# The block tile is read ahead of T, T's corner is transposed at a place of its own, and the inverse runs from 0.42 to 1.10 of a unit's period

## Chip, core and metric

The kernel runs on one core of one Trainium2 chip. The metric is the device time of one execution in microseconds (us), lower is better; the kernel before has a median of 692.04 us in three runs (691.59 to 693.32).

## What is computed

A linear attention with the delta rule runs over 768 steps for 4 batches of 8 heads (head size 48); its output, as 3072 tokens of width 384, goes through two dense layers with a squared ReLU between them. The core of the reference:

```python
k_n = k / (np.linalg.norm(k, axis=-1, keepdims=True) + 1e-06)
for t in range(S):
    kt, vt, bt = (k_n[:, :, t], v[:, :, t], beta[:, :, t, None])
    y[:, :, t] = np.einsum('bhd,bhde->bhe', q[:, :, t], state)
    v_old = np.einsum('bhde,bhd->bhe', state, kt)
    state = state + bt[:, :, :, None] * np.einsum('bhd,bhe->bhde', kt, vt - v_old)
...
h = np.maximum(x @ w_in, 0.0)
return (h * h @ w_out).astype(np.float32)
```

## The kernel before

**Units.** The 768 steps are cut into 12 units of 64 (`C`), for all 32 batch-head pairs at once. Inside a unit the recurrence is a triangular system: a 64x64 matrix T per head, the inverse of "identity plus masked key products", turns (v minus what the state gives) into the solved values. T consists of two 32x32 diagonal blocks and one 32x32 corner.

**Blocks and inverse.** `static` makes the masked key products of a unit (tile `ap`) and writes the four 32x32 diagonal parts to a DRAM tile `blocks` (`to_blocks`, L387). `from_blocks` (L397) reads them back in another layout as the block tile `lt`, 512 KB with one buffer; the same last piece of `static` issues the loads of v (L247) and beta (L274, L276). `invert` inverts the diagonal blocks on VectorE (DVE) in 31 elimination steps, each a product (L541) and a subtraction (L542) on the tile `z`, and a last multiplication by beta (L544). It writes `z` to DRAM (`inv`, L548) and, when that has landed, reads it back twice: as T's diagonal parts into `tt` (L552, 4 issues) and as the corner factor `t1t` (L557, 4 issues).

**The corner and the state.** `whole` makes T's corner. DVE transposes `t1t` into `t1` (L587); TensorE (PE) multiplies `ap` with `tt` (L594), ScalarE (ACT) copies that to `m` (L596), `keys_on_state` multiplies keys with the state (L633) and DVE subtracts the result from v (`vt`, L641). Then PE multiplies `t1` with `m` (L607), ACT writes the result to `tt` (L611), and `queries_on_state` follows (L633 again, output `g`). Later come `solved` (L657), `scores_on_solved` (L671) and `keys_on_solved` (L689), after which DVE updates the state (L694).

**The dense layers.** `moe` runs for the unit before: its first product is L750, its second L737; ACT applies ReLU, square and a rounding (L757, L758, L760), DVE forms the remainders `h_l` (L729) and `x_l` (L720). These matmuls fill TensorE while the recurrence's chain goes on.

**Order.** The schedule is manual: every engine runs its instructions in the order in which the Python code emits them. For each unit's period the parts are generators, each with a list of places between 0 and 1; `weave` sorts all places and advances one generator at each. In period u the inverse of unit u+1 begins at `I0` = 0.47 and ends at `I1` - 1 = 0.14 of the next period; its reads of `inv` stand at 0.16, the last piece of `static` for unit u+2 at 0.165. The chain `two_visits` has its first place at 17.5/32 (all of `whole`) and its second at 25.5/32 (`solved` and what follows). All DMAs named here are issued by one engine's queue, SyncE (SP), in order; SP waits at an issue until what it needs has come.

The lines of the main loop that set these places:

```python
begun = J0 if u == 1 else I0
n_i = round((1 - begun) / (I1 - begun) * NI)
...
    parts.append((ahead, [-1, 0.165]))
...
    parts.append((inverse, steps(n_i, begun, 1)))
    left = steps(NI - n_i, 0, I1 - 1) + [0.16]
...
parts.append((chain, [x / STEPS for x in (CHAIN if u > 1 else CHAIN1)]))
```

Of the kernel before, what the change touches and what calls it, by code (L numbers as in the profile page):

```python
# [8 lines left out]
F32 = mybir.dt.float32  # L9
# [12 lines left out]
def kernel(  # L22
# [22 lines left out]
    nc = tc.nc  # L45
    B, H, S, D = q.shape
    DM, DF = w_in.shape
    P = 128
    C = 64
    HB = 32  # L50
# [11 lines left out]
    apool = ctx.enter_context(tc.tile_pool(name="attn", bufs=2))  # L62
# [179 lines left out]
    def load_to(dst, x, d, width, queues=None):  # L242

        if x is v:
            for b, src in enumerate(tokens(x, d)):
                for c in range(NC):
                    nc.sync.dma_start(out=dst[b * C:(b + 1) * C, c], in_=src[:, c])  # L247
            return
        for j, queue in enumerate(queues or (nc.sync, nc.sync)):
            for b, src in enumerate(tokens(x, d)):  # L250
                rows = slice((b ^ j) * C, (b ^ j) * C + C)
                for c in range(NC):
                    queue.dma_start(out=dst[rows, c, j::2, :width], in_=src[:, c, j::2])
# [24 lines left out]
    def load_v(d):  # L278
        d["vt"] = apool.tile([P, NC, H, D], F32, name="vt", bufs=2)
        load_to(d["vt"], v, d, D)  # L280
# [31 lines left out]
    def x_tile(u=2):  # L312

        turn[0] += 1
        pool, name = (ps_h, "h") if u <= 1 and split_early and turn[0] % 4 >= 2 else (ps_x, "x")
        return pool.tile([P, PC], F32, name=name)


    def static(d):

        u = d["u"]
# [68 lines left out]
        def from_blocks(blocks):  # L390

            d["lt"] = lt = apool.tile([P, HB, HB], F32, name="lt", bufs=1)
            if u <= 1:
                nc.sync.dma_start(out=lt, in_=shared["blocks"].rearrange("n u h s t -> (n u h) s t"))
                return
            for g in range(2):
                nc.sync.dma_start(out=lt[g * C:(g + 1) * C], in_=blocks.rearrange("n h s t -> (n h) s t"))  # L397
# [45 lines left out]
        blocks = to_blocks()  # L443
        yield
        from_blocks(blocks)
        load_v(d)
        if u + 1 < MERGED:
            load_q(ds_[u + 1])
# [74 lines left out]
    def invert(d):  # L523
# [32 lines left out]
        for n in range(4):  # L556
            nc.sync.dma_start(out=t1t[n * HB:(n + 1) * HB], in_=inv[n // 2 * 2].rearrange("(k j) s t -> j s k t", j=2)[n % 2])  # L557

    def whole(d):

        u, ap = d["u"], d["ap"]
        tt = ttile[u % 2]
        upper = [slice(b * C, b * C + HB) for b in range(2)]
        lower = [slice(b * C + HB, (b + 1) * C) for b in range(2)]

        if not u:

            low, t1 = d["low"], d["t1"]
            m = mpool.tile([P, H2, HB], F32, name="x_l", bufs=1)
            ps = ps_h.tile([P, PC], F32, name="h").rearrange("p (h t) -> p h t", h=H2)  # L570
            for h in range(H2):
                for b in range(2):
                    nc.tensor.matmul(ps[upper[b], h], lhsT=ap[lower[b], h // H, h % H, 0, :HB], rhs=low[lower[b], h],
                                     start=True, stop=True)
            for b in range(2):
                nc.scalar.copy(out=m[upper[b]], in_=ps[upper[b]])
            yield
            ps = x_tile(u).rearrange("p (h t) -> p h t", h=H2)
            for h in range(H2):
                for b in range(2):  # L580
                    nc.tensor.matmul(ps[upper[b], h], lhsT=t1[upper[b], h], rhs=m[upper[b], h], start=True, stop=True)
            for b in range(2):
                nc.scalar.mul(out=tt.rearrange("p c h t -> p (c h) t")[upper[b], :, HB:], in_=ps[upper[b]], mul=-1.0)
            yield
            return
        t1 = apool.tile([P, H, HB], F32, name="t1", bufs=1)
        nc.vector.transpose(out=t1, in_=d["t1t"])  # L587
        m = apool.tile([P, H, HB], F32, name="m", bufs=1)
        at = [upper, lower]
        ps = ps_h.tile([P, PC], F32, name="h")[:, :H * HB].rearrange("p (k t) -> p k t", k=H)  # L590
        for h in range(H2):
            c, e = h // H, h % H
            for b in range(2):
                nc.tensor.matmul(ps[at[h % 2][b], h // 2], lhsT=ap[lower[b], c, e, 0, :HB],  # L594
                                 rhs=tt[lower[b], c, e, HB:], start=True, stop=True)
        nc.scalar.copy(out=m, in_=ps)  # L596
        if u == 1:
            yield
        keys_on_state(d)
        if u < MERGED - 2:  # L600
            yield
        ps = [(x_tile(u) if u < MERGED - 2 else ps_h.tile([P, PC], F32, name="h"))[:, :H * HB]
              .rearrange("p (k t) -> p k t", k=H) for _ in range(2)]
        for h in range(H2):
            for b in range(2):
                rows = at[h % 2][b]
                nc.tensor.matmul(ps[h % 2][upper[b], h // 2], lhsT=t1[rows, h // 2], rhs=m[rows, h // 2], start=True, stop=True)  # L607
        right = tt.rearrange("p c (k j) t -> p j (c k) t", j=2)
        for j in range(2):
            for b in range(2):  # L610
                nc.scalar.mul(out=right[upper[b], j, :, HB:], in_=ps[j][upper[b]], mul=-1.0)  # L611
        if u == 1:
            yield
        queries_on_state(d)
        yield
# [20 lines left out]
    def keys_on_state(d):  # L636

        ks = areas([x_tile() for _ in range(2)], NP)
        on_state(d, 0, ks)
        for left, old in zip(by_parity(d["vt"]), ks):  # L640
            nc.vector.tensor_tensor(out=left, in0=left, in1=old, op=ALU.subtract)  # L641
# [147 lines left out]
    def steps(n, a, b):  # L789

        return [a + (b - a) * (m + 0.5) / n for m in range(n)]
# [27 lines left out]
    def prepared(u):  # L819

        yield from static(ds_[u])
# [13 lines left out]
    def two_visits(d, ahead):  # L835

        ahead = ahead or iter(())
        for _ in whole(d):
            pass
        take(ahead, 1)  # L840
        yield
        solved(d)
        take(ahead, 1)
        scores_on_solved(d)
        take(ahead, 1)
        if d["u"] < units - 1:
            keys_on_solved(d)
        yield
# [1 line left out]
    STEPS = 32  # L850
    OVER = 4
    MERGED = 4
    CHAIN = (17.5, 25.5)
    CHAIN1 = (14.4, 17, 19.5, 21.5, 23.5, 27)
    L1, N1, N2 = 0.01, (0.36, 0.76), (0.03, 0.42)
    I0, I1, NI = 0.47, 1.14, HB
    J0 = 0.54
    units = S // C
    ds_ = []
    split_early = True  # L860
# [3 lines left out]
    with tc.manual_schedule(engines=engines):  # L864
# [74 lines left out]
        corner, inverse = inverse, None  # L939
        for u in range(1, units):  # L940
            parts = []
            begun = J0 if u == 1 else I0
            n_i = round((1 - begun) / (I1 - begun) * NI)
            if inverse:
                parts.append((inverse, left))
            getting, now = loads(u), moe(ds_[u - 1]) if u > 1 else first
            parts += [(now, [-2])] if u > 1 else []
            if u < MERGED - 1:
                parts.append((static(ds_[u + 1]), [-1, 0.155, 0.165] if u > 1 else [0.12, 0.2, 0.21]))
            elif ahead:  # L950
                parts.append((ahead, [-1, 0.165]))
            ahead = prepared(u + 2) if 1 < u < units - 2 else None
            inverse = invert(ds_[u + 1]) if u < units - 1 else None
            if inverse:
                parts.append((inverse, steps(n_i, begun, 1)))
                left = steps(NI - n_i, 0, I1 - 1) + [0.16]
            if u == 1:
                parts.append((corner, [0.04, 0.09, 0.1]))
                parts.append((third, [0.01, 0.015, 0.03, 0.045]))
                parts.append((late_loads(), [0.08]))  # L960
                parts.append((splits, steps(3 * (NW - FIRST) + 3 - used, 0, 0.72)))
                parts.append((pair[1], [0.25]))
            parts.append((getting, [L1] + steps(6, *N2) + [0.72, 0.93] if u + 2 < units else []) if u > 1 else
                         (getting, [0.09] + steps(6, *N1) + [0.93, 0.94]))
            chain = two_visits(ds_[u], ahead) if u > 1 else state_part(ds_[u])
            parts.append((chain, [x / STEPS for x in (CHAIN if u > 1 else CHAIN1)]))
            if before:
                parts += [(before, [x / STEPS for x in range(OVER)] + [0.2, 0.21])]
            parts.append((now, [x / STEPS for x in range(OVER, STEPS)] if u > 1 else steps(STEPS - OVER, 0, 1)))
            weave(*parts)  # L970
            before = now
# [34 lines left out]
```

## Time and profile before

| | us |
|---|---|
| median of three runs | 692.04 |
| the profiled execution, its own time | 693.88 |
| its span (first to last instruction) | 692.2 |
| TensorE busy in the span | 611.9 (88%) |
| VectorE busy | 425.8 (62%) |
| ScalarE busy | 317.5 (46%) |
[...]

[...] "Unit 7's corner" means the stretch from 404 to 430 us, in which T of unit 7 comes back and its corner is made; the corners of units 2 to 11 stand some 46 to 54 us apart from each other. A DVE entry of one line number repeats for each step. POOL is GpSimd.

### The profile page before, as it was taken

To read this page: it belongs to the slowest core of one execution; us is meant where nothing else is said; L and a number is where in the kernel's file an instruction comes from. 1 tells how busy PE (TensorE), PEld (TensorE's weight loads), DVE (VectorE), ACT (ScalarE), POOL (GpSimd) and SP (SyncE) were. 2 spreads that over 40 slices of the span, in tenths; PEclk is the share of its full clock that TensorE was granted. 3 is DMA by queue.
4 is the path that set the end of the run, shared out by engine and by line. 5 is a ranking of instruction groups with operands and counts; after the bars stand their busy time and mean duration, and the time that the engine had idled before them with its cause. 6 is when DMAs were issued, how large, how long until landed. Compare 5 with 4: busy or idle time off the path is not lost.

```text
span 692.2 us, 23846 instructions
## 1 busy us (share of the span) xinstructions
PE 611.9 (88%) x10392; PEld 581.9 (84%) x10392; DVE 425.8 (62%) x1131; ACT 317.5 (46%) x621; POOL 29.8 (4%) x52
## 2 busy tenths in 40 slices
PE   2858798998997997997997997997997998998997
PEld 2456787998897997996997997997997998898997
DVE  4796698864864774774684684684685574651121
ACT  5648576544443444443453443453444343444352
POOL 4000100010010010010010010010010010000000
PEclk9957899998997998997998998997998998999999
DMA  7788552253144135135135235235135024020000
GB/s 230 173 260 222 118 99 38 42 99 65 26 74 82 26 59 94 29 54 96 32 48 98 36 47 97 38 48 95 34 48 92 3 42 91 3 46 19 24 1 24
DMA packets 172464, 49.32 MB, mean 71 GB/s; under 512 B 164288, under 2 KB 167368, under 8 KB 172360
## 3 DMA queue, kind: packets, MB, share of 16 engines
q1 hardware_dynamic: 168840, 47.06, 33.8%
q8 instruction: 82, 1.34, 0.8%
q10 hardware_dynamic: 3392, 0.72, 0.6%
q14 instruction: 22, 0.18, 0.1%
q0 software_dynamic: 128, 0.01, 0.0%
HBM read 36.54 MB, written 10.49 MB: 68 GB/s over the span
## 4 chain that ended last, share of the span: by engine, by line
PE 47%; DVE 19%; DMA 13%; SPq 10%; ACT 7%; issue 4%; ACTq 0%; DVEq 0%
PE o L737 18%; PE h L750 15%; DVE tmp L541 5%; DVE z L542 4%; DMA vt<-in_v_dram 4%; DMA inv<-z 4%; PE g L633 3%; SPq L557 3%; SPq L247 2%; DVE ap L379 2%; SPq L552 2%; PE g L671 2%; PE x L353 2%; DVE state L694 2%; DMA w<-in_moe_w_in_dram 2%
## 5 line engine op out<-in xcount | busy, mean ns | idle before, releaser
L737 PE MATMUL o<-w,h_h 128*128 128x384 f32 x768 | 209.1, 355 | 0.0
L750 PE MATMUL h<-x_h,w 128*128 128x256 f32 x1152 | 169.3, 283 | 0.0
L757 ACT ACTIVATE r<-h 128x512 f32<-128x512 f32 x96 | 57.5, 599 | 236.4 <-PE h L750 234.3
L729 DVE TENSOR_TENSOR h_l<-r,h_h 128x512 fp32r<-128x512 f32 x96 | 66.1, 689 | 146.9 <-ACT h_h L760 146.8
L750 PEld LDWEIGHTS h<-x_h,w 128*128 128x128 f32 x1152 | 155.4, 190 | 0.7
L737 PEld LDWEIGHTS o<-w,h_h 128*128 128x128 f32 x768 | 142.0, 197 | 2.6
L737 PE MATMUL o<-w,h_l 128*128 128x384 f32 x384 | 133.4, 347 | 0.0
L541 DVE SCALAR_TENSOR_TENSOR tmp<-lt,bt,z 128x126 f32<-128x126 f32 (+22 forms) x310 | 97.4, 314 | 47.7 <-DMA lt<-blocks 35.6
L750 PE MATMUL h<-x_l,w 128*128 128x256 f32 x576 | 99.9, 282 | 0.0
L542 DVE TENSOR_TENSOR z<-z,tmp 128x126 f32<-128x126 f32 (+22 forms) x310 | 79.2, 255 | 10.6
L750 PEld LDWEIGHTS h<-x_l,w 128*128 128x128 f32 x576 | 82.2, 190 | 0.0
L737 PEld LDWEIGHTS o<-w,h_l 128*128 128x128 f32 x384 | 75.2, 196 | 0.0
L758 ACT ACTIVATE r<-r 128x512 f32<-128x512 f32 x96 | 60.7, 632 | 3.1
L760 ACT CAST h_h<-r 128x512 fp32r<-128x512 f32 x96 | 59.5, 620 | 3.1
L607 PE MATMUL h<-m,t 32*32 32x32 f32 x640 | 10.3, 227 | 33.9 <-DVE t L587 33.0
L607 PEld LDWEIGHTS h<-m,t 32*32 32x32 f32 x640 | 9.1, 139 | 35.0 <-issue 34.4
L611 ACT ACTIVATE tt<-h 32x256 f32<-32x256 f32 x40 | 15.0, 374 | 39.7 <-PE h L607 39.2
L530 POOL MEMSET z<- 128x512 f32 x10 | 5.5, 546 | 505.5 <-DMA inv<-z 350.4
L694 DVE TENSOR_TENSOR state<-state,x 48x384 f32<-48x384 f32 x40 | 22.0, 550 | 3.7 <-PE x L689 3.1
L671 PE MATMUL g<-vt,ap 64*64 64x48 f32 x768 | 17.3, 221 | 6.4 <-ACT vt L659 5.4
L671 PEld LDWEIGHTS g<-vt,ap 64*64 64x64 f32 x768 | 14.5, 134 | 9.1 <-ACT vt L659 8.6
L633 PE MATMUL g<-state,kq 48*64 48x48 f32 x704 | 20.6, 290 | 1.4 <-issue 1.4
(147 smaller groups left out, 672.7 us busy)
## 6 DMA issues: line engine op xcount, KB each, us to landing
w<-in_moe_w_in_dram SPq DMA_DIRECT2D x12, 512.0 KB
w<-in_moe_w_out_dram SPq DMA_DIRECT2D x16, 384.0 KB
lt<-blocks SPq DMA_DIRECT2D x20, 256.0 KB
qpad<-in_q_dram SPq DMA_DIRECT2D x96, 48.0 KB
vt<-in_v_dram SPq DMA_DIRECT2D x48, 96.0 KB
out_dram<-a SPq DMA_DIRECT2D x46, 96.0 KB
kpad<-in_k_dram SPq DMA_DIRECT2D x88, 48.0 KB
blocks<-ap SPq DMA_DIRECT2D x40, 64.0 KB
```

The lines of the kernel that those rows point to most:

```text
L541: nc.vector.scalar_tensor_tensor(out=tmp, scalar=bt[:, s:s + 1], op0=ALU.mult, op1=ALU.mult, **factors)
L542: nc.vector.tensor_tensor(out=z[:, :nj, s + 1:], in0=z[:, :nj, s + 1:], in1=tmp, op=ALU.subtract)
L557: nc.sync.dma_start(out=t1t[n * HB:(n + 1) * HB], in_=inv[n // 2 * 2].rearrange("(k j) s t -> j s k t", j=2)[n % 2])
L633: nc.tensor.matmul(dst[j][to, c, p], lhsT=d["kq"][rows, c, p, b, x], rhs=state[rows, b, c, p], start=(c == 0 and p == 0) if x else True, s ...
L671: nc.tensor.matmul(gy[j][to, c, p], lhsT=ap[rows, c, h, 1], rhs=uu[rows, c, h], start=(u == 0 and c == 0 and p == 0), stop=True, skip_grou ...
L694: nc.vector.tensor_tensor(out=state[rows, b], in0=state[rows, b], in1=ku[b][rows], op=ALU.add)
L729: nc.vector.tensor_tensor(out=h_l, in0=r, in1=h_h.bitcast(F32), op=ALU.subtract)
L737: nc.tensor.matmul(o[i], lhsT=a[:, e, i * P:(i + 1) * P], rhs=halves["wo", ft][w], start=(ft == 0 and n == 0), stop=(ft == FT - 1 and n == 2))
L750: nc.tensor.matmul(hp[:, e], lhsT=halves["wi", (kt, ft // EACH)][w][:, f], rhs=x[:, kt], start=(n == 0), stop=(n == 3 * KT - 1))
L757: nc.scalar.activation(out=r, in_=hp, func=AF.Relu)
L758: nc.scalar.activation(out=r, in_=r, func=AF.Square)
L760: nc.scalar.copy(out=h_h, in_=r)
```

## The change

Three things are edited, all of them places in an order; no arithmetic is changed. (1) The last piece of `static` for units from 2 on is split: the read of the block tile is one piece, the loads of v, q and beta the next. The reads now stand at 0.13 of a period, the loads at 0.17, and T's reads at 0.15 (0.16 in period 2), so from unit 3 on SP issues the block tile ahead of T. (2) The transposition of `t1t` is a function of its own, `corner_rows`, that `two_visits` calls at a new place 15.5/32, before `whole` at 17.5/32. (3) The inverse begins at 0.42 and ends at 1.10 of a period (0.5 and 1.12 in period 2; 0.54 and 1.14 in period 1, as before).

```diff
         from_blocks(blocks)
+        yield
         load_v(d)
...
+    def corner_rows(d):
+
+        d["t1"] = apool.tile([P, H, HB], F32, name="t1", bufs=1)
+        nc.vector.transpose(out=d["t1"], in_=d["t1t"])
+        return d["t1"]
+
     def whole(d):
...
-        t1 = apool.tile([P, H, HB], F32, name="t1", bufs=1)
-        nc.vector.transpose(out=t1, in_=d["t1t"])
+        t1 = d["t1"] if "t1" in d else corner_rows(d)
...
         ahead = ahead or iter(())
+        corner_rows(d)
+        yield
         for _ in whole(d):
...
-    CHAIN = (17.5, 25.5)
+    CHAIN = (15.5, 17.5, 25.5)
...
-    I0, I1, NI = 0.47, 1.14, HB
-    J0 = 0.54
+    NI, SPANS = HB, {1: (0.54, 1.14), 2: (0.5, 1.12)}
...
-            begun = J0 if u == 1 else I0
-            n_i = round((1 - begun) / (I1 - begun) * NI)
+            begun, ended = SPANS.get(u, (0.42, 1.1))
+            n_i = round((1 - begun) / (ended - begun) * NI)
...
-                parts.append((static(ds_[u + 1]), [-1, 0.155, 0.165] if u > 1 else [0.12, 0.2, 0.21]))
+                parts.append((static(ds_[u + 1]), [-1, 0.155, 0.165, 0.17] if u > 1 else [0.12, 0.2, 0.21, 0.215]))
...
-                parts.append((ahead, [-1, 0.165]))
+                parts.append((ahead, [-1, 0.13, 0.17]))
...
-                left = steps(NI - n_i, 0, I1 - 1) + [0.16]
+                left = steps(NI - n_i, 0, ended - 1) + [0.16 if u == 1 else 0.15]
```

Line numbers behind the edits shift by up to 7 (L541 becomes L542, L552 becomes L553, L729 becomes L735). The order of TensorE, ScalarE and GpSimd is the same in both kernels. Two engines get another order.

**SP, the issues of one unit** (units 3 to 10 alike): `inv` is the write of the inverse, `tt` and `t1t` are T's reads, `lt` is the block tile of the next unit. Before:

```order
L548 DMA inv<-z 1024x1x32 x2
L552 DMA tt_108<-inv 32x16x32 x4
L557 DMA t1t<-inv 32x8x32 x4
L397 DMA lt<-blocks 64x1024 x2
L247 DMA vt<-in_v_dram 64x8x48 x4
```

After:

```order
L549 DMA inv<-z 1024x1x32 x2
L397 DMA lt<-blocks 64x1024 x2
L553 DMA tt_108<-inv 32x16x32 x4
L558 DMA t1t<-inv 32x8x32 x4
L247 DMA vt<-in_v_dram 64x8x48 x4
```

The two issues of `lt` moved from behind T's eight to a place between the write and T's first read.

**DVE, from the first step of the next inverse to the remainder behind the corner** (units 3 to 9 alike). The pairs on `tmp` and `z` are the steps, `STREAM_TRANSPOSE` is the corner's, `vt` is the subtraction of `keys_on_state`. Before:

```order
L729 TENSOR_TENSOR h_l<-r,h_h 128x512
L541 SCALAR_TENSOR_TENSOR tmp<-lt,bt,z 128x31
L542 TENSOR_TENSOR z<-z,tmp 128x31
L541 SCALAR_TENSOR_TENSOR tmp<-lt,bt,z 128x30
L542 TENSOR_TENSOR z<-z,tmp 128x30
L541 SCALAR_TENSOR_TENSOR tmp<-lt,bt,z 128x58
L542 TENSOR_TENSOR z<-z,tmp 128x2x29
L541 SCALAR_TENSOR_TENSOR tmp<-lt,bt,z 128x56
L542 TENSOR_TENSOR z<-z,tmp 128x2x28
L587 STREAM_TRANSPOSE t_5868<-t1t 128x256
L641 TENSOR_TENSOR vt<-vt,x 128x8x48 x2
L729 TENSOR_TENSOR h_l<-r,h_h 128x512
```

After:

```order
L735 TENSOR_TENSOR h_l<-r,h_h 128x512
L542 SCALAR_TENSOR_TENSOR tmp<-lt,bt,z 128x30
L543 TENSOR_TENSOR z<-z,tmp 128x30
L542 SCALAR_TENSOR_TENSOR tmp<-lt,bt,z 128x58
L543 TENSOR_TENSOR z<-z,tmp 128x2x29
L563 STREAM_TRANSPOSE t_5841<-t1t 128x256
L542 SCALAR_TENSOR_TENSOR tmp<-lt,bt,z 128x56
L543 TENSOR_TENSOR z<-z,tmp 128x2x28
L542 SCALAR_TENSOR_TENSOR tmp<-lt,bt,z 128x81
L543 TENSOR_TENSOR z<-z,tmp 128x3x27
L542 SCALAR_TENSOR_TENSOR tmp<-lt,bt,z 128x78
L543 TENSOR_TENSOR z<-z,tmp 128x3x26
```

The first step now stands ahead of the remainder `h_l`, the transposition behind three steps instead of four, and three further steps stand between it and the subtraction `vt`. For unit 2 the transposition stands ahead of every step.

**DVE, behind the mask of the next unit** (units 3 to 9 alike): `ap` is the first mask, `state` the update, and the steps behind them are those that remain of this inverse. Before:

```order
L379 TENSOR_TENSOR ap<-h,mask 128x4x128 x2
L694 TENSOR_TENSOR state<-state,x 48x384 x4
L541 SCALAR_TENSOR_TENSOR tmp<-lt,bt,z 128x128
L542 TENSOR_TENSOR z<-z,tmp 128x8x16
L729 TENSOR_TENSOR h_l<-r,h_h 128x512
```

After:

```order
L379 TENSOR_TENSOR ap<-h,mask 128x4x128 x2
L700 TENSOR_TENSOR state<-state,x 48x384 x4
L735 TENSOR_TENSOR h_l<-r,h_h 128x512
L542 SCALAR_TENSOR_TENSOR tmp<-lt,bt,z 128x130
L543 TENSOR_TENSOR z<-z,tmp 128x10x13
```

The three largest steps (128, 135 and 126 elements) moved ahead of the mask: 13 steps remain behind it, where there were 16. The inverse's last multiplication (L544) also moved, from behind the two sums of squares (L297) of the next normalisation to ahead of them.

## Rows read from the trace of the kernel before

**Rows 1.** The page: busy time of TensorE, share of the span, instructions

```profile
PE 611.9 (88%) x10392; PEld 581.9 (84%) x10392; DVE 425.8 (62%) x1131; ACT 317.5 (46%) x621; POOL 29.8 (4%) x52
```

**Rows 2.** Waits of all engines: engine, line, waited for; total us, times, longest

```profile
DVE tmp L541 <- DMA lt<-blocks: 35.6, 8, 5.2
...
PE h L607 <- DVE t L587: 33.0, 9, 4.5
```

**Rows 3.** Timeline of PE around unit 7's corner: start, us, operation, [idle before]

```profile
418.58 0.76 PE L594 MATMUL h<-tt,ap 32*32 32x32 f32 x64
419.27 1.15 PE L633 MATMUL x<-state,kq 48*64 48x48 f32 x64
424.47 1.07 PE L607 MATMUL h<-m,t 32*32 32x32 f32 x64 [4.06 <-DVE t L587]
425.48 1.96 PE L633 MATMUL g<-state,kq 48*64 48x48 f32 x64
...
429.27 0.62 PE L737 MATMUL o<-w,h_h 128*128 128x384 f32 x2
```

**Rows 4.** Timeline of DVE, same place

```profile
416.38 0.69 DVE L729 TENSOR_TENSOR h_l<-r,h_h 128x512 fp32r<-128x512 f32 x1 [0.72 <-ACT h_h L760]
421.80 0.25 DVE L541 SCALAR_TENSOR_TENSOR tmp<-lt,bt,z 128x31 f32<-128x31 f32 x1 [4.73 <-DMA lt<-blocks]
...
423.88 0.45 DVE L587 STREAM_TRANSPOSE t<-t1t 128x256 f32<-128x256 f32 x1
```

**Rows 5.** Timeline of SP's DMA issues, same place

```profile
408.41 1.27 SPq L548 DMA_DIRECT2D inv<-z  x2
...
413.99 2.85 SPq L557 DMA_DIRECT2D t1t<-inv  x4
416.88 1.13 SPq L397 DMA_DIRECT2D lt<-blocks  x2
```

**Rows 6.** Timeline of ACT, same place: the copy that the product reads

```profile
420.50 0.37 ACT L596 COPY m<-h 128x256 f32<-128x256 f32 x1
```

**Rows 7.** Timeline of DVE: the inverse between the first mask and its last product

```profile
390.05 1.29 DVE L379 TENSOR_TENSOR ap<-h,mask 128x512 f32<-128x512 f32 x2 [2.07 <-PE g L671]
...
406.75 1.00 DVE L297 TENSOR_REDUCE n<-rest 128x8 f32<-128x384 f32 x2
407.67 0.68 DVE L544 TENSOR_TENSOR z<-z,bt 128x512 f32<-128x512 f32 x1
```

**Rows 8.** Unit 11, with no block tile to read: timelines of PE, DVE, SP

```profile
626.48 0.75 PE L607 MATMUL h<-m,t 32*32 32x32 f32 x64 [0.51 <-ACT m L596]
627.17 1.07 PE L633 MATMUL g<-state,kq 48*64 48x48 f32 x57
629.30 0.33 PE L633 MATMUL g<-state,kq 48*64 48x48 f32 x7 [1.07 <-issue]
...
623.37 0.45 DVE L587 STREAM_TRANSPOSE t<-t1t 128x256 f32<-128x256 f32 x1 [0.74 <-DMA t1t<-inv]
...
613.06 1.25 SPq L548 DMA_DIRECT2D inv<-z  x2
```

**Rows 9.** One microsecond each: busy of PE, PEld, DVE, ACT, POOL, granted clock, DMA

```profile
160.00:161.00 1.00, 0.79 (x26) 0.72 (x26) 0.93 (x4) 0.96 (x3) 0.00 (x0) 0.50 0.00 0
...
422.00:423.00 1.00, 0.00 (x0) 0.00 (x0) 0.86 (x5) 0.00 (x0) 0.00 (x0) 0.72 0.96 114
...
628.00:629.00 1.00, 0.24 (x17) 0.17 (x8) 0.00 (x0) 0.76 (x3) 0.00 (x0) 1.00 0.00 0
```

**Rows 10.** Chain that ended last: the twelve output products after a corner

```profile
164.26 3.31 PE o L737 x12
...
583.10 3.76 PE o L737 x12
...
629.63 2.32 PE o L737 x12
```

**Rows 11.** Timeline of PE: unit 2's corner, after the shortest wait

```profile
159.09 0.79 PE L607 MATMUL h<-m,t 32*32 32x32 f32 x62 [2.17 <-DVE t L587]
```

## The prediction

> **What bounds the kernel now.** I read the page first: TensorE is busy for 88% of the span [rows 1], so what is to be won lies in the time in which it waits, and in the time in which it runs at the lower clock. Next the waits: one line carries nearly all of TensorE's waiting in the steady part, the corner product L607, which waits nine times (units 2 to 10) for DVE's transposition, 33.0 us in all; beside it DVE waits eight times for the block tile, 35.6 us [rows 2]. The timelines of one corner show that these are one event. PE ends its product on the state at 419.27 + 1.15 = 420.42 and starts L607 at 424.47, idle for 4.06 [rows 3]. DVE, free after its remainder at 416.38 + 0.69 = 417.07, stands for 4.73 at the first step of the next inverse, until the block tile has come at 421.80; then four steps run, 2.08 in all, 0.52 a step, and only then, at 423.88, comes the transposition, 0.45 [rows 4]. The corner factor itself was issued from 413.99, ahead of the block tile from 416.88 [rows 5], so the transposition waits for steps that it doesn't need, and these for a tile that is read last. After the idle time the granted clock falls to half: it averages 0.72 from 422 to 423 [rows 9], and the products on the state that took 1.15 before the wait take 1.96 behind it, the corner product 1.07 [rows 3]. Unit 11 is the counter-example in the same trace. There no block tile is read and no step stands ahead: the corner product waits 0.51, for ACT's copy m, it takes 0.75, and the clock is still 1.00 two microseconds later [rows 8, 9].
>
> **The wait.** What is late next when the transposition is early? ACT's copy: m ends at 420.50 + 0.37 = 420.87 [rows 6], 0.45 behind PE's own end at 420.42; unit 11 shows the same with 0.51 [rows 8]. I take 0.51. Now the two conditions for it.
>
> DVE's place. The first step stands ahead of the remainder that ends at 417.07; before it DVE was idle for 0.72 [rows 4], which covers a step of 0.52. Two more steps follow, 1.04: the transposition's place comes at 418.1, and it would end at 418.6, 2.3 before m.
>
> T's arrival. The inverse's tail gets shorter. From the first mask at 390.05 to the end of the last multiplication at 407.67 + 0.68 = 408.35 DVE runs nearly without a pause [rows 7]; the mask's start is set by PE. Three steps leave this stretch, at least 3 x 0.52 = 1.6 (the large ones take more), and the sums of squares, 0.92 from 406.75 to 407.67 [rows 7], go behind the multiplication: 2.5 in all. So T's write is issued at 405.9 instead of 408.41 [rows 5]. From that issue to the corner factor's landing unit 11 needs 623.37 - 613.06 = 10.3, without a block tile in front [rows 8]. The block tile needs 421.80 - 416.88 = 4.9 from its first issue [rows 4, 5]. Its cost to T lies between nothing (it moves while SP waits for the write to land) and all of its 4.9. The factor lands at 416.2 or, at worst, at 421.1. In the first case the transposition finds it there; in the second it ends at 421.6, and PE's wait is 1.2 to 1.3 rather than 0.5, 0.8 x 8 = 6.4 more in the sum. I take the first: the write's landing holds SP in any case, and the block tile can use that time.
> [...] No run here shows a large read queued in front of T.
>
> Sum of the first term: 33.0 for nine waits become 9 x 0.51 = 4.6, a gain of 28.4.
>
> **The clock.** If the wait is 0.5, the clock should stay up, as it does in unit 11. What the lower clock costs is read from the same operations on both sides. Corner product: 1.07 against 0.75 [rows 3, 8], 0.32 x 8 = 2.6 (unit 2's ran mostly before the fall, 0.79 [rows 11]). Products of the queries: 1.96 against 1.15 [rows 3], 0.81 x 9 = 7.3. The transposes of keys and queries in units 2 to 9 run from 427.44, the end of those products, to 429.27, 1.8 [rows 3], at half clock; the two pairs above shrink to 0.70 and 0.59, so they should save 0.55 to 0.75, and I take 0.6 x 8 = 4.8. The first twelve output products after the corner: nine such rows, the first 3.31 and the last 3.76, with the sum 30.02; at the full clock they take 2.32 [rows 10]: 30.0 - 20.9 = 9.2. Together 23.9.
>
> **What comes up in its place.** In unit 11, right behind the corner without a long wait, PE stands for 1.07 at "issue" in the middle of the products of the queries [rows 8]: four products of 64 small matmuls each follow one another there. Where PE stood for 4 us just before, the row of unit 7 has no such gap [rows 3]. It may come back in all nine units, 9 x 1.07 = 9.6, or in none. I take 0.6 each, 5.4.
> [...] The trace shows 1.07 and names no more than "issue" for it.
>
> **Edits with no price.** The extra yields issue nothing. The loads of v, q and beta stay behind T. The subtraction of vt has three more steps in front, 1.6: with the transposition at 418.6 it can start when PE's products on the state end at 420.42 and is done some 1.0 later, while the x bank it frees is wanted again after the corner product and the products of the queries, 0.75 + 1.15 behind 420.9: this cover is 1.4. The remainder behind it moves by a step. No instruction is added, and DVE's load leaves room in a shorter period: it waits some 4.7 at this one place of each period [rows 4].
>
> **The sum.** 28.4 + 23.9 - 5.4 = 46.9 from 693.88 gives 647.0 for such an execution; the profiled one lay 1.84 above the median, so 645.1 as a median: I say 645. With no gap 640; with the full gap, T at its worse end or a part of the clock's gain lost, 655.
>
> **Rivals.**
> *The clock falls anyway.* The wait goes, but small matmuls, a wait of 0.5 and a gap of 1.07 stand close together, and the transposes of small tiles follow, which unit 11 doesn't have. For it: a wait of 2.17 in unit 2 was enough [rows 11], the clock is 0.50 from 160 on [rows 9]. Against it: unit 11's 0.51 and 1.07 together left it at 1.00 [rows 8, 9]. Then only 28.4 - 5.4 = 23.0 is won: 669 as a median.
> *The wait changes its name.* T is late behind the block tile, and the change doesn't remove the wait but halves it: 2.2 in eight units and 0.5 in unit 2 make 18.1, with the clock lost as in unit 2 [rows 9, 11]. Won: 14.9; 677 as a median. It needs T 5 to 6 later than my estimate, more than the whole 4.9 of the block tile. At the extreme T comes just as late as the transposition does now: no change, 692.
> *Slower: DVE's queue stands at the transposition.* Its place is earlier, so if the factor isn't there, DVE holds up behind it three steps, the subtraction of vt, the next remainder and with them the whole inverse of the next unit, which sets the next T. The point is where the transposition would start later than now, 423.88: when the factor lands 18.0 after T's write is issued (423.88 - 405.9), 7.7 more than unit 11's 10.3. Each further microsecond costs 8 units one each: with 19.2, 1.2 x 8 = 9.6, 702 as a median. Against it: the block tile accounts for 4.9 at most.
>
> **How the numbers follow.** Forecast 0.75 (640 to 655); clock falls anyway 0.10 (664 to 670); wait halved 0.07 (677); no change 0.03; slower 0.05 (702). Range: 638 to 668 takes in the forecast with its bounds and about half of the second case; 0.20 stays outside. A measurement tells about 0.3%, 2.1 us, from no change: faster 0.92, same 0.03, slower 0.05.
>
> **What would show it.** Right: the wait of L607 for DVE is gone from the waits and one of about 0.5 for ACT's m stands there; the granted clock stays at 1.00 through the corner; the products of the queries take 1.1 to 1.2; corners lie 5.2 (46.9 / 9) closer together on average; DVE's wait for the block tile shrinks to little; the write of T comes 2 to 3 earlier against the mask. Wrong in part: L607 waits for the transposition and that for the corner factor's DMA (T behind the block tile), or products of 1.9 with no wait of DVE before them (clock), or gaps at "issue" of more than 1 in each unit. Wrong altogether: DVE idle at the transposition for over 5 us in each unit, with T's write later in each period than now.

## The result and the profile after

| | before | after |
|---|---|---|
| median, us | 691.85 | 663.5 |
| lowest to highest | 691.59 to 693.32 | 661.13 to 667.99 |
| profiled execution, its own time | 693.88 | 661.13 |
| its span | 692.2 | 659.4 |
| mean granted clock of TensorE, as a share of the full clock | 0.924 | 0.951 |

The ratio is 0.9594, 95% interval 0.9535 to 0.9652: the changed kernel is faster by 4.1%. The forecast was 645 with a range of 638 to 668; the direction was right and the time lies in the range, but in the upper part, 18.5 above the likeliest value.

First the waits of the changed kernel, in the same columns as [rows 2]:

```profile
PE h L613 <- issue: 5.1, 5, 1.5
...
PE h L613 <- ACT m L602: 4.8, 10, 0.5
...
PE g L639 <- issue: 4.5, 5, 1.1
...
DVE tmp L542 <- DMA lt<-blocks: 2.6, 1, 2.6
```

The 33.0 us for DVE's transposition are gone. In their place stand 4.8 for ACT's copy `m`, ten times 0.5, as unit 11 showed it before the change [rows 8]; DVE's 35.6 for the block tile are 2.6, all of it in one unit. Grown are the two rows with "issue": five gaps in the corner product (L613) and five in the products of the queries (L639), where the kernel before had 0.3 in one gap and 1.4 in two, the 1.07 of unit 11 [rows 8] among them.

Unit 7's corner again, now near 400 us, in the timelines of PE, DVE and SP (against [rows 3 to 5]; DVE's rows at 372 and 387 answer to [rows 7]):

```profile
400.88 0.78 PE L600 MATMUL h<-tt,ap 32*32 32x32 f32 x64
401.58 1.15 PE L639 MATMUL x<-state,kq 48*64 48x48 f32 x64
403.22 0.75 PE L613 MATMUL h<-m,t 32*32 32x32 f32 x64 [0.49 <-ACT m L602]
403.90 1.13 PE L639 MATMUL g<-state,kq 48*64 48x48 f32 x60
406.01 0.32 PE L639 MATMUL g<-state,kq 48*64 48x48 f32 x4 [0.97 <-issue]
406.25 0.46 PE L353 MATMUL x<-plus,kpad 64*128 64x64 f32 x8
...
407.40 0.62 PE L743 MATMUL o<-w,h_h 128*128 128x384 f32 x2
...
372.33 1.29 DVE L379 TENSOR_TENSOR ap<-h,mask 128x512 f32<-128x512 f32 x2 [1.32 <-PE g L677]
...
387.11 0.69 DVE L545 TENSOR_TENSOR z<-z,bt 128x512 f32<-128x512 f32 x1
...
400.29 0.45 DVE L563 STREAM_TRANSPOSE t<-t1t 128x256 f32<-128x256 f32 x1
...
387.86 1.27 SPq L549 DMA_DIRECT2D inv<-z  x2
389.31 1.35 SPq L397 DMA_DIRECT2D lt<-blocks  x2
391.50 1.90 SPq L553 DMA_DIRECT2D tt<-inv  x4
393.44 1.97 SPq L558 DMA_DIRECT2D t1t<-inv  x4
```

The transposition starts at 400.29 without idle time in front, and the corner product 0.49 behind the products on the state. The products of the queries then run at full speed (60 in 1.13) until a gap of 0.97; the transposes of keys and queries take 1.15, from 406.25 to 407.40, where they took 1.8. T's write is issued 387.86 - 372.33 = 15.5 behind the mask; before it was 408.41 - 390.05 = 18.4. SP's first read of T comes 3.6 behind that write, with two issues of the block tile between them, and it came 3.6 behind it before as well: 412.04, behind 408.41.

The last view is the granted clock, as a share of the full one (1.00). The periods between corner products of the changed kernel (columns: start and end; length; busy time of PE, PEld, DVE, ACT and POOL in us, each with its count of instructions; granted clock; DMA share; GB/s):

```profile
158.07:207.41 49.34, 46.87 (x829) 45.31 (x829) 36.21 (x105) 22.32 (x43) 1.96 (x3) 0.97 0.35 64
207.41:255.18 47.77, 45.70 (x828) 44.15 (x828) 34.07 (x95) 22.32 (x43) 2.29 (x3) 1.00 0.35 66
255.18:305.48 50.30, 48.34 (x828) 46.82 (x828) 33.86 (x95) 22.32 (x43) 2.49 (x3) 0.93 0.34 62
305.48:355.67 50.19, 48.27 (x829) 46.75 (x829) 34.14 (x96) 22.31 (x43) 2.28 (x3) 0.93 0.33 63
...
403.22:451.06 47.84, 45.71 (x829) 44.16 (x829) 34.08 (x96) 22.32 (x43) 2.29 (x3) 1.00 0.35 66
...
546.00:593.64 47.64, 44.90 (x701) 43.57 (x701) 25.43 (x71) 19.32 (x36) 0.00 (x0) 0.93 0.14 26
```

Five of the nine periods from unit 2 to unit 11 have 1.00 (two of them are shown) and last 47.4 to 47.8; the two after units 4 and 5 have 0.93 and last 50.3 and 50.2. Unit 2's has 0.97, unit 10's, which has fewer matmuls, 0.93. Inside, at unit 4 (one microsecond each; of the engines PE alone):

```profile
256.00:257.00 1.00, 0.07 (x3) 0.98 0.00 0
257.00:258.00 1.00, 1.00 (x36) 0.50 0.06 8
...
262.00:263.00 1.00, 1.00 (x4) 0.50 0.46 89
```

The clock is 0.50 from 257 on, behind the gap of the corner product, and has not come back at 262. In the profiled execution it fell to 0.50 at units 2, 4, 5 and 10. In unit 7 of the kernel before, with PE idle from 420.42 to 424.47, it averaged 0.72 from 422 to 423 [rows 9] and was 0.50 from 423 to 429.

### The profile page after: what moved, and what is told of

Read it like the earlier page. It is cut to its first block, busy times and chain, and to the rows that moved or that the text cites. A ratio compares the mean times of both kernels' runs of the same rounds, so it can differ in the third digit from the quotient of the medians.

```text
span 659.4 us, 23855 instructions
## 1 busy us (share of the span) xinstructions
PE 601.3 (91%) x10392; PEld 570.6 (87%) x10392; DVE 426.2 (65%) x1131; ACT 317.2 (48%) x621; POOL 30.8 (5%) x52
## 4 chain that ended last, share of the span: by engine, by line
PE 80%; ACT 10%; issue 4%; DMA 3%; DVE 2%; SPq 1%; ACTq 0%; DVEq 0%
PE o L743 32%; PE h L756 31%; PE g L639 2%; PE x L369 2%; ACT r L764 2%; PE g L677 2%; ACT r L763 2%; ACT h_h L766 2%; PE x L353 1%; PE h L613 1%; PE x L695 1%; DMA kpad<-in_k_dram 1%; ACT vt L665 1%; PE h L722 1%; PE h L353 1%
## 5 line engine op out<-in xcount | busy, mean ns | idle before, releaser
L743 PE MATMUL o<-w,h_h 128*128 128x384 f32 x768 | 205.9, 350 | 0.0
L735 DVE TENSOR_TENSOR h_l<-r,h_h 128x512 fp32r<-128x512 f32 x96 | 68.3, 711 | 150.9 <-ACT h_h L766 150.3
L756 PEld LDWEIGHTS h<-x_h,w 128*128 128x128 f32 x1152 | 157.1, 192 | 0.6
L743 PEld LDWEIGHTS o<-w,h_h 128*128 128x128 f32 x768 | 139.0, 193 | 2.4
L542 DVE SCALAR_TENSOR_TENSOR tmp<-lt,bt,z 128x126 f32<-128x126 f32 (+22 forms) x310 | 96.8, 312 | 10.9 <-DMA lt<-blocks 2.6
L677 PE MATMUL g<-vt,ap 64*64 64x48 f32 x768 | 17.7, 221 | 7.7 <-ACT vt L665 5.4
L356 ACT COPY kq<-x 128x512 f32<-128x512 f32 x25 | 13.6, 592 | 16.1 <-PE x L353 16.1
L369 PE MATMUL x<-kq 48*64 48x64 f32 (+1 forms) x608 | 19.5, 256 | 1.2 <-ACT kq L356 0.7
L639 PE MATMUL g<-state,kq 48*64 48x48 f32 x704 | 16.0, 237 | 4.5 <-issue 4.5
```

Source lines behind the costliest of these rows:

```text
L369: nc.tensor.matmul(ps[j][to * C:(to + 1) * C, p, (x - first) * C:(x - first + m) * C], lhsT=kq[rows, c, p, b, 0], rhs=kq[rows, c, p, b, x: ...
L542: nc.vector.scalar_tensor_tensor(out=tmp, scalar=bt[:, s:s + 1], op0=ALU.mult, op1=ALU.mult, **factors)
L639: nc.tensor.matmul(dst[j][to, c, p], lhsT=d["kq"][rows, c, p, b, x], rhs=state[rows, b, c, p], start=(c == 0 and p == 0) if x else True, s ...
L677: nc.tensor.matmul(gy[j][to, c, p], lhsT=ap[rows, c, h, 1], rhs=uu[rows, c, h], start=(u == 0 and c == 0 and p == 0), stop=True, skip_grou ...
L735: nc.vector.tensor_tensor(out=h_l, in0=r, in1=h_h.bitcast(F32), op=ALU.subtract)
L743: nc.tensor.matmul(o[i], lhsT=a[:, e, i * P:(i + 1) * P], rhs=halves["wo", ft][w], start=(ft == 0 and n == 0), stop=(ft == FT - 1 and n == 2))
```

## Experiments

The theories. **A**: the block tile, read last, holds the steps ahead of the transposition; its place is what matters, and its passage costs T little. Rivals: T itself is late, or the other edits bring the gain. **C** (formed from the trace after): what lies between the forecast and the result is the lower clock, which follows the wait for `m` and the gap at "issue"; large matmuls put ahead of them should take them away, and the clock should then stay up. Its rival **D**: something steady, such as the corner's chain, is the bound. The ratios are to the kernel before, timed beside each run on the same chip.

| run | edit | median, us | ratio (95%) |
|---|---|---|---|
| tile_first | before + block tile ahead of T | 666.4 | 0.9606 (0.9552 to 0.9661) |
| corner_place | before + own place for the transposition | 684.6 | 0.9865 (0.9822 to 0.9908) |
| inverse_early | before + inverse from 0.42 to 1.10 | 693.7 | 1.0 (0.9967 to 1.0034) |
| tile_last | after, block tile behind T again | 681.0 | 0.9806 (0.976 to 0.9851) |
| after_again | after | 665.5 | 0.9609 (0.9565 to 0.9653) |
| dense_before_corner | after + 12 dense products ahead of the corner product | 645.9 | 0.9303 (0.926 to 0.9345) |
| dense_after_corner | after + the 12 behind it | 662.8 | 0.9559 (0.9522 to 0.9596) |
| dense_both | after + 6 ahead and 6 behind | 650.9 | 0.9387 (0.9352 to 0.9422) |
| dense_then_keys_later | dense_before_corner + transposes of the next keys later | 642.1 | 0.9251 (0.9209 to 0.9293) |
| tile_first_dense | tile_first + the 12 ahead | 645.9 | 0.9308 (0.9283 to 0.9333) |
| before_dense | before + the 12 ahead | 667.8 | 0.9625 (0.9589 to 0.9661) |

### The three edits one by one

**tile_first**, on the kernel before:

```diff
         from_blocks(blocks)
+        yield
         load_v(d)
...
-                parts.append((ahead, [-1, 0.165]))
+                parts.append((ahead, [-1, 0.15, 0.17]))
```

> The kernel before with one edit: the block tile is issued between the write of T and T's reads; the transposition and the inverse stay where they were. Theory A (the block tile's late arrival holds the steps ahead of the transposition, and its passage costs T little): the four steps run right behind the remainder that ends 3.4 us before PE's own end, the transposition is over before ACT's copy m, so the corner product waits 0.5 in units 3 to 10 and still 2.2 in unit 2, 8 x 3.4 = 27 won on waits plus some clock, 660 to 668. Rival B (the tile's whole passage of 4.9 us goes into T's, whose write is not earlier here): the corner factor lands 15.2 after the write is issued, the wait is 3.6, about 688.

Measured 666.4, within theory A's figures; the rival's 688 is out. The timelines of unit 7 on SP, DVE and PE:

```profile
390.02 1.27 SPq L549 DMA_DIRECT2D inv<-z  x2
391.47 1.27 SPq L397 DMA_DIRECT2D lt<-blocks  x2
...
395.56 1.97 SPq L558 DMA_DIRECT2D t1t<-inv  x4
...
397.69 0.69 DVE L730 TENSOR_TENSOR h_l<-r,h_h 128x512 fp32r<-128x512 f32 x1 [1.07 <-ACT h_h L761]
398.30 0.25 DVE L542 SCALAR_TENSOR_TENSOR tmp<-lt,bt,z 128x31 f32<-128x31 f32 x1
...
400.38 0.45 DVE L588 STREAM_TRANSPOSE t<-t1t 128x256 f32<-128x256 f32 x1
...
402.24 0.86 PE L608 MATMUL h<-m,t 32*32 32x32 f32 x64 [0.51 <-ACT m L597]
...
405.27 0.32 PE L634 MATMUL g<-state,kq 48*64 48x48 f32 x4 [1.11 <-issue]
```

Four steps run from 398.30 right behind the remainder, and the transposition starts at 400.38 with no idle time. So the corner factor had landed by then, at most 400.38 - 390.02 = 10.4 behind T's write, with 512 KB queued in front of it; without them unit 11 needed 10.3 [rows 8]. The tile's passage cost T nothing that shows: the lower end of the prediction's 0 to 4.9. The DMA moved 105, 142, 278 and 263 GB/s in the four microseconds from 391 to 395, some 788 KB, about T's write (256 KB) and the tile (512 KB) together, so by an estimate from these bytes the tile was nearly through when SP issued the corner factor's reads at 395.56. Unit 2, whose order is unchanged, still waits 2.1 for the transposition, as it did.

**corner_place**, on the kernel before: `corner_rows` as in the change, called in `two_visits` ahead of `whole`, and its place.

```diff
-    CHAIN = (17.5, 25.5)
+    CHAIN = (15.5, 17.5, 25.5)
```

> The kernel before with one edit: the transposition at its own place 15.5/32, so that one step of the next inverse stands ahead of it instead of four; block tile last, inverse as before. Theory A: the transposition still waits for the block tile through that one step, but three steps of 0.52 less; the wait of the corner product falls from 4.06 to 2.5, 9 x 1.6 = 14 won, the clock still falls, 676 to 680. Rival (the corner factor's own landing releases the transposition): no change, 692.

Measured 684.6, 1.3% faster with an interval clear of 1, so the factor's own landing is not what released the transposition, but 5 to 9 short of what was expected. The waits:

```profile
DVE tmp L541 <- DMA lt<-blocks: 34.9, 8, 5.2
...
PE h L612 <- DVE tmp L541: 17.7, 8, 2.9
...
PE h L612 <- issue: 5.1, 4, 1.8
```

The mechanism is as expected: the block tile is still waited for (34.9), and the corner product waits 17.7 / 8 = 2.2 in units 3 to 10, rather than (33.0 - 2.17) / 8 = 3.9. What was left out are the gaps at "issue", 5.1 in the corner product alone; behind the longer waits of the kernel before there was 0.3.

**inverse_early**, on the kernel before:

```diff
-    I0, I1, NI = 0.47, 1.14, HB
-    J0 = 0.54
+    NI, SPANS = HB, {1: (0.54, 1.14), 2: (0.5, 1.12)}
```

(and `begun`, `ended` and `left` as in the change.)

> The kernel before with one edit: the inverse from 0.42 to 1.10 of a period. Theory A: T's write and with it T and the block tile come 2.5 to 2.8 us earlier against the mask, but six steps instead of four stand between the block tile and the transposition, 1.2 more; the wait of the corner product falls from 4.06 to about 2.6, 8 x 1.45 + 1.1 = 12.7 won, the clock still falls, 677 to 681. Rival (the stretch behind the mask sets nothing, since PE sets the mask): wait 5.2, 8 x 1.2 = 10 lost, 702.

Measured 693.7, ratio 1.0: both were wrong. DVE at unit 7's corner, the mask ahead of it and T's write on SP:

```profile
390.60 1.29 DVE L379 TENSOR_TENSOR ap<-h,mask 128x512 f32<-128x512 f32 x2 [1.30 <-PE g L671]
...
405.38 0.69 DVE L544 TENSOR_TENSOR z<-z,bt 128x512 f32<-128x512 f32 x1
...
419.22 0.25 DVE L541 SCALAR_TENSOR_TENSOR tmp<-lt,bt,z 128x31 f32<-128x31 f32 x1 [4.25 <-DMA lt<-blocks]
...
422.98 0.45 DVE L587 STREAM_TRANSPOSE t<-t1t 128x256 f32<-128x256 f32 x1
...
406.14 1.27 SPq L548 DMA_DIRECT2D inv<-z  x2
```

T's write comes 406.14 - 390.60 = 15.5 behind the mask, 2.8 sooner, as expected. But from the tile's landing at 419.22 to the transposition at 422.98 pass 3.76, where it was 2.08: besides two more steps a remainder `h_l` of 0.68 stands there too, behind the first step. The waits for the transposition sum to 28.6 instead of 33.0, the gaps at "issue" in the corner product and the queries' products to 3.2 instead of 1.7, and the clock is the same (0.923 and 0.924). The profiled execution is 2.1 shorter than the one before (691.78 and 693.88), but of that the median of ten runs shows nothing: by itself this edit brings nothing that could be measured.

**tile_last**, on the changed kernel:

```diff
-                parts.append((ahead, [-1, 0.13, 0.17]))
+                parts.append((ahead, [-1, 0.165, 0.17]))
```

> The changed kernel with one edit undone: the block tile is issued behind T's reads again. Theory A: the tile lands 2.5 to 2.8 earlier than in the kernel before, three steps run and the transposition ends about 1.0 us behind PE's own end, so the wait is 1.0 instead of 0.5: 8 x 0.5 = 4 more than the changed kernel, and the clock falls more often, 666 to 674. Rival (the place of the tile is what brings the gain): the wait is 3 or more, 685 and up.

Measured 681.0, between the two. DVE at unit 8's corner, and T's write and the block tile on SP:

```profile
462.46 0.25 DVE L542 SCALAR_TENSOR_TENSOR tmp<-lt,bt,z 128x31 f32<-128x31 f32 x1 [4.70 <-DMA lt<-blocks]
...
462.85 0.69 DVE L735 TENSOR_TENSOR h_l<-r,h_h 128x512 fp32r<-128x512 f32 x1
...
464.45 0.45 DVE L563 STREAM_TRANSPOSE t<-t1t 128x256 f32<-128x256 f32 x1
...
448.38 1.26 SPq L549 DMA_DIRECT2D inv<-z  x2
...
457.39 1.13 SPq L397 DMA_DIRECT2D lt<-blocks  x2
```

DVE waits 4.70 for the tile, and the remainder is held behind the first step again, ahead of the transposition; the tile came 462.46 - 448.38 = 14.1 behind the write, 0.7 more than in the kernel before (421.80 - 408.41). The wait of the corner product is 13.8 in seven units, 2.0 each, not 1.0. With all else in the change kept, the tile's place is worth some 14 to 17 us (14 and 15 by the ratios, 15.5 and 17.5 by the medians); alone it gives 0.9606, the whole change 0.9594 and 0.9609. On top of the tile's place the two other edits bring nothing that could be measured; without it they bring this run's 0.9806.

### The clock and the gap

**after_again**: the changed kernel, unedited.

> The changed kernel once more, beside the next three on the same chip. Theory C (what keeps it above the forecast is the lower clock, which follows the wait of 0.5 for m and the gap of about 1.0 at issue in some units and not in others): the time moves from run to run with the granted clock, 661 to 668. Rival (something steady, DVE or the DMAs): runs agree within 1 us.

Five runs from 659.0 to 667.6, so something steady, with runs within 1 us, is out. In order of length: 659.0, 663.8, 665.5, 665.9 and 667.6; their mean granted clocks: 0.953, 0.946, 0.949, 0.942 and 0.941. The fastest has the highest clock and the two slowest the lowest: the spread goes with the clock, if not one to one (663.8 and 665.5 are the other way round). In the profiled one the clock fell to 0.50 at units 2, 4, 8 and 10, not the same four as in the first.

**dense_before_corner**, on the changed kernel: `whole` yields behind `keys_on_state` in every unit, and two pieces of the dense layers are woven in there.

```diff
         keys_on_state(d)
-        if u < MERGED - 2:
-            yield
+        yield
...
-        for _ in whole(d):
-            pass
+        at = whole(d)
+        for x in range(STOPS):
+            next(at)
+            yield
+        take(at)
         take(ahead, 1)
...
-    CHAIN = (15.5, 17.5, 25.5)
+    CHAIN = (15.5, 17.5, 19.5, 25.5)
+    STOPS = 1
```

> The changed kernel with twelve output products of the dense layers (2.1 us) between PE's products on the state and the corner product, in units 2 to 11. [...] Rival D (the corner's chain is the bound, so what is put in front of the corner product delays all that follows): 2.1 x 10 more, about 684.

Theory C came to 24 less than the changed kernel, 638 to 645: nine waits of 0.5, gaps of 8.9 and four falls of the clock of 2.7 each. Measured 645.9, 1 above that range and 18 to 20 below the changed kernel, and D with its 684 is out. PE's waits from 150 to 610 us, in full, and its timeline at unit 3:

```profile
PE h L755 <- ACT kq L356: 8.0, 8, 1.1
PE g L676 <- ACT vt L664: 5.4, 10, 1.3
PE x L694 <- issue: 0.3, 1, 0.3
...
205.05 1.15 PE L638 MATMUL x<-state,kq 48*64 48x48 f32 x64
206.13 0.62 PE L742 MATMUL o<-w,h_h 128*128 128x384 f32 x2
...
208.44 0.75 PE L612 MATMUL h<-m,t 32*32 32x32 f32 x64
209.12 1.15 PE L638 MATMUL g<-state,kq 48*64 48x48 f32 x64
...
212.56 0.98 PE L755 MATMUL h<-x_h,w 128*128 128x256 f32 x6 [1.05 <-ACT kq L356]
```

No wait for `m`, no gap in the corner product or the queries' products, and the clock stays at 1.00 from 150 to 640 us. A new wait of 1.0 in eight units stands instead: the first dense product behind the transposes of the next keys waits for ACT's copies of them, because the twelve products that used to cover those copies now stand ahead of the corner. How much of these 8.0 can be had back, dense_then_keys_later shows.

**dense_after_corner**, the same with the `yield` behind the corner product instead of ahead of it:

```diff
-        if u == 1:
-            yield
+        yield
         queries_on_state(d)
```

> The changed kernel with the same twelve output products behind the corner product, ahead of the products of the queries. Theory C: the wait for m stays at 0.5; the gap goes only in the units where it stood in the products of the queries, every second one (4 to 5 us); the clock falls less often: 650 to 660. Rival D: no change or 2.1 x 10 more.

Measured 662.8, a little above the range expected. The gap goes in every second unit, as theory C has it: five gaps in the corner product, 6.2 in all, and none in the products of the queries. The copies' wait (9.1) is the part that was not counted. The clock fell to 0.50 at units 2, 6 and 10, each of them a unit with a gap; in the five units with the wait for `m` but no gap (3, 5, 7, 9 and 11) it stayed at 1.00. It didn't fall in units 4 and 8 either, which have both.

**dense_both**, with both yields, `CHAIN = (15.5, 17.5, 18.5, 19.5, 25.5)` and `STOPS = 2`:

> The changed kernel with six output products ahead of the corner product and six behind it. Theory C: the wait for m is hidden by 1.06 us of products, the gap is nearly gone (1.0 less 1.06 in one half of the units, less 2.1 in the other), the clock stays up: 638 to 648. Rival D: about 10 to 20 more than the changed kernel.

Measured 650.9, 3 above the range expected. Gaps of 0.2 to 1.1 are left in five units (2.8 in all), the wait for `m` is gone, and the clock stays at 1.00 from 150 to 640 us. The copies cost 9.2 here as well.

**dense_then_keys_later**, on dense_before_corner:

```diff
         take(at)
+        yield
         take(ahead, 1)
...
-    CHAIN = (15.5, 17.5, 19.5, 25.5)
+    CHAIN = (15.5, 17.5, 19.5, 21.5, 25.5)
```

> The changed kernel with twelve output products ahead of the corner product, and with the transposes of the next keys and queries two pieces of the dense layers later (behind 18 first-layer products). Theory C: the twelve products cost a new wait of 1.0 in eight units, for ACT's copies of those transposes, since nothing dense stood behind them; with them later it goes, 8.0 less than with the transposes in place, 636 to 640, and the corners lie 46.2 apart. Rival (PE waits for the same copies wherever the transposes stand, or the scores wait for late keys): 645 to 650.

Measured 642.1, 2 above the expected range, the fastest of all, and 3.8 below dense_before_corner where 8.0 were expected. PE's waits from 150 to 610 us, in full:

```profile
PE g L676 <- ACT vt L664: 5.4, 10, 1.3
PE g L676 <- issue: 0.6, 2, 0.4
PE x L694 <- issue: 0.2, 1, 0.2
```

The copies' wait is gone, but only part of it came back as time: from unit 2's corner to unit 10's it is 372.3, in dense_before_corner 377.0, 4.7 less, while PE is busy for 367.9 there rather than 365.3; the runs don't show why. The corners of units 2 to 10 lie 46.1 to 46.8 apart, where the forecast for the change came to some 47. What PE still waits for is the copy of the solved values, 5.4.

**tile_first_dense**, tile_first with the `yield` of dense_before_corner and `CHAIN = (17.5, 19.5, 25.5)`:

> The kernel before with the block tile ahead of T and twelve output products ahead of the corner product; transposition and inverse as in the kernel before. Theory A with C (the tile's place and the dense products are all that matters; the two other edits only take 2 us off unit 2, which the products now cover): 644 to 648, like the changed kernel with the products. Rival (the earlier inverse or the own place of the transposition is needed once the period is shorter): 655 and up.

Measured 645.9, the same as with the other two edits in. Neither the transposition's own place nor the earlier inverse is needed, even at this shorter period.

**before_dense**, the same on the kernel before, without the block tile's move:

> The kernel before with the twelve output products ahead of the corner product and nothing else. Theory A: the wait of 4.06 for the transposition is covered by 2.1 of products, 1.9 remains in eight units, 33.0 becomes 15, the transposes' new wait of 1.0 in eight units comes on top: 10 won, the clock falls in some units only, 670 to 682. Rival (the dense products alone bring what they bring in the changed kernel): 655 or less.

Measured 667.8: the rival's 655 is out; 2 better than the expected range. The wait for the transposition is 12.3 in eight units, 1.5 each, and the copies take 7.5:

```profile
PE h L606 <- DVE t L587: 12.3, 8, 2.1
```

Twelve products put into the wait bring here nearly as much as the tile's move does (667.8 and 666.4); the two together bring 645.9.

## Why the prediction was right, and where its sizes were off

**The wait: right in place, cause and size.** Nine waits for the transposition, 33.0, became waits of 0.5 for `m` (predicted 0.51). tile_first, corner_place and tile_last show the block tile to be the cause.

**T's arrival: right at the end that was taken.** The tail is 2.8 shorter (predicted at least 2.5), and a block tile queued in front cost T nothing that shows (10.4 against 10.3). The worse bound of 4.9 did not come about: SP issues its first read of T 3.6 behind the write, the corner factor's reads later still, and by then, by the estimate from the bytes moved in tile_first, the tile was nearly through.

**The gap: the term was mis-sized.** Predicted 0.6 a unit, 5.4, from one row of 1.07. In the trace after, units 2 to 10 have 1.54, 1.15, 1.03, 0.99, 0.81, 0.97, 0.84, 0.76 and 0.86, 8.95 in all: the one row was the right price for each. The sum took all of it as new, but the kernel before had 0.6 in units 2 and 5. Its other corners, with long waits and the lower clock behind them, had none; which of the two kept the gaps away no run separates.

**The clock: this is the step that failed in size.** "If the wait is 0.5, the clock should stay up, as it does in unit 11" held in five units of nine. At units 2, 4, 5 and 10 it fell. The periods behind the first three are 49.3, 50.3 and 50.2 against 47.4 to 47.8 of the undisturbed ones; less their gaps they are longer by some 1.1, 2.6 and 2.5. The one behind unit 10 lasts 47.64, and dense_then_keys_later has 43.37 there, without the wait of 0.5 and the gap of 0.86, so some 2.9. Together some 9. The corners lie 3.5 closer together on average, not 5.2.

The shortfall can be counted without these estimates. From unit 2's corner to unit 11's PE was idle for 37.65 before and 18.65 after, 19.0 less, where wait and gap together were to give 28.4 - 5.4 = 23.0. It was busy for 429.74 before and 416.92 after, 12.8 less, where the clock was to give 23.9. So 11.1 are missing in the time of the work and 4.0 in the idle time; ahead of unit 2's corner the run after was 1.0 shorter, which leaves the 14.1 that lie between the sum's 647.0 and the profiled 661.13. The four falls make up some 9 of the 11.1; the other 2 stay open, and may mean that 23.9 was too much for the clock (a slip in it, 30.0 - 20.9 as 9.2, is only 0.1).

The rival "the clock falls anyway" was thus partly true: it was set up as all or nothing, and the kernel does it in some units, other ones in each run. The median of 663.5 lies nearer to this rival's 669 than to the forecast's 645; that it lies in the range is owed to the half of this rival that the range took in.

**What is shown and what is not.** Shown: with wait and gap both taken out by dense products the clock stays up in every corner (dense_before_corner), with only the wait taken out as well (dense_both), and with the wait alone left it stays up too (the gapless units of dense_after_corner). In all three, large matmuls also stand in the middle of the small ones, so it isn't shown whether the wait and the gap bring the clock down or the long stretch of small matmuls with them. Not settled either: which of the units that have both will fall. Unit 3 of the changed kernel, with 0.51 and 1.15, kept its clock; unit 10, with 0.42 and 0.86, lost it.

## What to carry to other kernels

Read first what is waited for last: here one read put ahead of T's eight in its queue gave all that could be measured of the change, and a shorter chain in front of T's write by itself gave nothing. When a long wait of TensorE is to go, ask what it has been hiding; where the clock fell at a short wait and a short gap among small matmuls (units 4, 5 and 10 here), the lower clock cost some 2.5 to 2.9, the wait and the gap themselves 1.3 to 1.5. A run of large matmuls that is due anyway can be moved into such a place, and then one must look for what it used to cover.

## What was not expected of the hardware

The gaps at "issue" stand at the same places every second unit: behind 60 of the 64 corner products in units 4, 6, 8 and 10, behind 60 of the 64 products of the queries in units 3, 5, 7 and 9. A period has 828 or 829 matmuls and as many weight loads; from one gap to the next it is 64 pairs more or less than that. The trace says only "issue" there, and what holds PE at these places no run shows. The gaps, among matmuls of 32*32 and 48*64, are 0.8 to 1.5 us in units 2 to 10, and with 2.1 us of large matmuls ahead of the corner product (dense_before_corner) they are gone.
